# Scattering the lists of experts 2 to 7 earlier, reading them a step later, and products on TensorE that nobody reads

## The chip, the cores and the metric

The kernel runs on one core of one Trainium2 chip. The metric is the device time of one execution in microseconds; several timed runs give a median.

## The reference

Three stages follow each other. The input is a batch of 4 sequences of 448 tokens with 12 heads of 64 (1792 tokens of 768 values).

```python
# attention, per head: q, k normalised by their root mean square, softmax, times v
x = attention(q, k, v)                     # [1792, 768]
# first mixture of experts, 8 experts, cap = 1792 / 8 = 224 tokens each
order = argsort(-(x @ w_gate).flatten())   # best (token, expert) pairs first
for tok, e in order:                       # a token goes to the first expert with room
    if assigned[tok] < 0 and counts[e] < cap: assigned[tok] = e; counts[e] += 1
for e in range(8): out[assigned == e] = relu(x[assigned == e] @ w1[e]) @ w2[e]
# second mixture: expert = argmax(x @ w_gate2 + bias[modality]), any count,
# rows scaled by the softmax weight of the chosen expert
```

## The kernel before, in words

Attention writes its rows to a table x_d in DRAM. Then comes the routing of the first mixture: a search by rounds for one threshold for each expert (`one_round`), after which `choose` writes the 0/1 matrix `Dm` (token by expert) and `ranks` writes `rk`, each token's place in its expert's list. `judge` counts the tokens of each expert and writes a flag. Code behind `tc.If(f1 > 0)` (line 1005) repairs the choice where the flag is set; every engine reads the flag and passes the branch. With these inputs the body isn't run.

The lists say which tokens an expert gets. Those of experts 0 and 1 are worked out on TensorE: `slots1` compares `rk` with the slot numbers on VectorE, `slots2` multiplies by token numbers on TensorE, and `gather1` has GpSimd fetch the 224 rows of x by two indirect DMAs. Those of experts 2 to 7 go through DRAM: `lists` (five VectorE operations) turns `rk` and `Dm` into positions `pos1`; `lists_go` has GpSimd scatter (token, modality) pairs, one indirect DMA for each of the 16 chunks of 112 tokens, into three zeroed tables `l1_d` in turn (`c % 3`), so that a scatter writes the same table as the third before it and waits for it; `list_load` has SyncE read the three tables back, and VectorE add them to `idx` and `inf`.

The experts then run one after the other, a step `u` for each: 8 steps of the first mixture, then steps of the second over tiles of tokens. A step has 16 chunks. Chunks 0 to 7 are `layer1` (18 products of 224 columns each in split precision, into one of three PSUM tiles `ph`), chunks 8 to 15 are `layer2`. Between them an order written out by hand places everything else: `at(u, c, f)` runs f after the products of chunk c of step u and ahead of their copies out of PSUM (`layer1_end`, `layer2_end`), and with `late=True` behind these copies. Each engine runs its instructions in that order. So placed are the weight loads on SyncE (`w_load`, four buffers `raw`), their splits into high and low parts on ScalarE and VectorE (`w_split`), the gathers, the transposes of the next step's rows into `xs` (`x_turn`, chunks 10 to 15), and the routing of the second mixture.

Just ahead of step 0, behind `judge`, VectorE has the six low parts of w1 (line 1003 with 806), then the branch, then its share of `x_turn(0)`.

In the order of before the lines that matter here are:

```python
at(0, 3, slots2, 1, oh1)
at(0, 3, lists, late=True)
at(0, 5, lists_go, 0, 8)
at(0, 8, lists_go, 8, NCH)
at(0, 15, list_load)
...
cg = 4                      # chunk of gather(1) in step 0; gather(2) is at chunk 3 of step 1
```

Of the kernel before, what the change touches and what calls it, by code (L numbers as in the profile page):

```python
# [8 lines left out]
FT = mybir.dt.float32  # L9
FR = mybir.dt.float32r  # L10
HF = mybir.dt.float16
I32 = mybir.dt.int32
AF = mybir.ActivationFunctionType
OP = mybir.AluOpType
# [13 lines left out]
def build(ctx, tc, q, k, v, g_q, g_k, m1_gate, m1_w1, m1_w2, modality, m2_gate, m2_bias, m2_w1, m2_w2,  # L28
# [5 lines left out]
    P = 112  # L34
# [911 lines left out]
    def gather1(e):  # L946
        for t in range(2):
            nc.gpsimd.indirect_dma_start(out=XG[e][:P, t], out_offset=None, in_=x_d,
                                         in_offset=bass.IndirectOffsetOnAxis(ap=IDX[e][:, t, 0:1], axis=0))
# [4 lines left out]
        IDX[e], INF[e] = idx[:, 2 * e:2 * e + 2], inf[:, 2 * e:2 * e + 2]  # L954


    XR2 = []

    def rows_last(c):
# [36 lines left out]
    slots(0)  # L996
    XG[0] = io.tile([128, 2, HD], FT, name="xg")
    gather1(0)
    judge(0)
    nc.vector.tensor_reduce(add4, ident.rearrange("p (a c) -> p c a", a=4)[:, :E], axis=AX.X, op=OP.add)  # L1000
    nc.vector.memset(flag_i[:, 1:3], 0)
    for i in range(DJ):
# [2 lines left out]
    with tc.If(f1 > 0):  # L1005
        with tc.For_i(0, 4, 1) as _i:
            one_round()
        choose()
        judge(1)
        f2 = nc.values_load(flag_i[0:1, 1:2], min_val=0, max_val=4096)  # L1010
        with tc.If(f2 > 0):
            for f in spread(NCH, mm, mc, mcb, sm[:, 0], lambda: ps1.tile([128, 512], FT, name="ph")):
                f()
            with tc.For_i(0, 40, 1) as _i:
                one_round()
            choose()
            judge(2)
            f3 = nc.values_load(flag_i[0:1, 2:3], min_val=0, max_val=4096)
            with tc.If(f3 > 0):

                fid = rr.tile([P, NCH, E], FT, name="fid")
                for b in range(B):
                    nc.gpsimd.iota(fid[:, b * CPB:(b + 1) * CPB], pattern=[[E, CPB], [1, E]], base=b * S * E,
                                   channel_multiplier=CPB * E, allow_small_or_imprecise_dtypes=True)
                nc.vector.tensor_copy(vv, lg)
                nc.vector.memset(Dm, 0.0)
                cnt = sm[:, 0, :]
                nc.vector.memset(cnt, 0.0)
                col = rr.tile([P, 4], FT, name="col")
                row = rr.tile([1, P], FT, name="row")  # L1030
                one = rr.tile([1, 1], FT, name="one")
                hs = rr.tile([P, E], HF, name="hs")

                def top(src, c):

                    p1 = ps1.tile([128, 512], FT, name="ph")
                    nc.tensor.transpose(p1[:1, :P], src, ident[:P, :P])
                    nc.vector.tensor_reduce(one, p1[:1, :P], axis=AX.X, op=OP.max)
                    nc.vector.tensor_copy(row, one.to_broadcast([1, P]))
                    p2 = ps1.tile([128, 512], FT, name="ph")  # L1040
                    nc.tensor.matmul(p2[:P, 0:1], row, ident[0:1, 0:1], start=True, stop=True)
                    nc.vector.tensor_copy(col[:, c:c + 1], p2[:P, 0:1])

                with tc.For_i(0, N, 1) as _i:
                    fl2 = vv.rearrange("p c e -> p (c e)")
                    nc.vector.tensor_reduce(col[:, 0:1], fl2, axis=AX.X, op=OP.max)
                    top(col[:, 0:1], 1)
                    nc.vector.tensor_scalar(lt0, vv, col[:, 1:2], None, op0=OP.is_equal)
                    nc.vector.tensor_scalar(uu, fid, -1.0, 20000.0, op0=OP.mult, op1=OP.add)
                    nc.vector.tensor_mul(uu, uu, lt0)  # L1050
                    nc.vector.tensor_reduce(col[:, 2:3], uu.rearrange("p c e -> p (c e)"), axis=AX.X, op=OP.max)
                    top(col[:, 2:3], 3)
                    nc.vector.tensor_scalar(lt0, uu, col[:, 3:4], None, op0=OP.is_equal)
                    nc.vector.tensor_add(Dm, Dm, lt0)
                    nc.vector.tensor_reduce(mx, lt0, axis=AX.X, op=OP.max)
                    nc.vector.tensor_scalar(mx, mx, -2e38, 1e38, op0=OP.mult, op1=OP.add)
                    nc.vector.tensor_tensor(vv, vv, mx[:, :, None].to_broadcast([P, NCH, E]), op=OP.min)
                    nc.vector.tensor_reduce(sm[:, 1, :], lt0.rearrange("p c e -> p e c"), axis=AX.X, op=OP.add)
                    nc.vector.tensor_copy(hs, sm[:, 1, :])
                    p3 = ps1.tile([128, 512], FT, name="ph")  # L1060
                    nc.tensor.matmul(p3[:, :E], ones_h[:P], hs, start=True, stop=True)
                    nc.vector.tensor_add(cnt, cnt, p3[:P, :E])
                    full = sm[:, 2, :]
                    nc.vector.tensor_scalar(full, cnt, float(cap) - 0.5, None, op0=OP.is_gt)
                    nc.vector.tensor_scalar(full, full, -2e38, 1e38, op0=OP.mult, op1=OP.add)
                    nc.vector.tensor_tensor(vv, vv, full[:, None, :].to_broadcast([P, NCH, E]), op=OP.min)
        ranks()
        slots(0)
        gather1(0)
    rr_st.close()  # L1070


# [109 lines left out]
            layer2_end(u, c - 8)  # L1182
        run(16 * u + c, True)


    pos1 = act.tile([P, NCH], I32, name="p3i")

    def lists():
        p3 = act.tile([P, NCH, E], FT, name="p3")
        ps = act.tile([P, NCH], FT, name="p3s")  # L1190
        e224 = act.tile([P, 1, E], FT, name="e224")
        nc.vector.tensor_scalar(e224, eio[:P], float(cap), -1.0, op0=OP.mult, op1=OP.add)
        nc.vector.tensor_add(p3, rk, e224.to_broadcast([P, NCH, E]))
        nc.vector.tensor_mul(p3, p3, Dm)
        nc.vector.tensor_reduce(ps, p3, axis=AX.X, op=OP.add)
        nc.vector.tensor_copy(pos1, ps)

    def lists_go(a, b):
        for c in range(a, b):

# [10 lines left out]
    def slots_next(a):  # L1211
# [2 lines left out]
            OH.append(act.tile([P, HD], mybir.dt.bfloat16, name="junk").bitcast(HF))  # L1214
        slots1(1, a, a + 4, oh1)

    def list_load():
        l3 = act.tile([P, 3, 2 * E, 2], I32, name="l3")
        for g in range(3):
            nc.sync.dma_start(l3[:, g, 4:], l1_d[g][2 * cap:].rearrange("(t p) f -> p t f", p=P))  # L1220
        nc.vector.tensor_add(l3[:, 0, 4:], l3[:, 0, 4:], l3[:, 1, 4:])
        nc.vector.tensor_add(idx[:, 4:], l3[:, 0, 4:], l3[:, 2, 4:])
        nc.vector.tensor_copy(inf[:, 4:], idx[:, 4:, 1])
# [211 lines left out]
    for u in range(US):  # L1435
        if u < E:
            W[u] = (m1_w1[u], m1_w2[u])
            at(u, 3 if u == E - 1 else 9, route_bias, u)
        for p in range(3, 7):
            for i in range(2):  # L1440
                c = 2 * (p - 3) + i
                at(u, c, w_split, u, p, i, nc.vector)
        nx = u + 1
        if u == 0:
            for p in range(4, 7):
                at(0, -1, w_load, 0, p)
            for i in range(4):
                at(0, i // 2, slots_next, 4 * i, late=True)
            at(0, 3, slots2, 1, oh1)
            at(0, 3, lists, late=True)  # L1450
            at(0, 5, lists_go, 0, 8)
            at(0, 8, lists_go, 8, NCH)
            at(0, 15, list_load)
        if u < E:
            route(u)
        if u in (E - 2, E - 1):
            if u == E - 2:
                at(u, 0, tile_consts)
            at(u, 9, tile_pick, u - E + 2, late=True)
        if u == E:  # L1460
            for i, f in enumerate(tile_rest()):
                at(u, 7 + i // 5, f, late=True)
        if nx == US:
            break

        cv, cw, cs, cg, cx = None, (1, 3, 5), (8, 8, 9, 10, 10, 11), 3, range(10, 16)
        if u == 0:
            cg = 4
        elif nx >= E:
            cv = 0  # L1470
        if cv is not None:
            j = nx - E - NP0 - (NT0 if nx in SHORT else 0)
            at(u, cv, tile_values, nx, slice(j, j + 1))
        for p in range(3):
            at(u, cw[p], w_load, nx, p)
        if cv is not None:
            at(u, cw[0], tile_list, nx)
            at(u, cg, tile_gather, nx)
        else:
            at(u, cg, gather, nx)  # L1480
        at(u, max(7, cw[2]), w_load, nx, 3)
        for p in range(3):
            for i in range(2):
                at(u, cs[2 * p + i], w_split, nx, p, i, nc.vector)
            at(u, min(15, cs[2 * p + 1] + 1), w_load, nx, 4 + p)
        for j in range(DJ):
            at(u, cx[j], x_turn, nx, j)
# [53 lines left out]
```

## Time and profile before

| | us |
|---|---|
| median of three timed runs | 889.77 (886.84 to 889.78) |
| the profiled execution | 888.51 |
| its span in the profile | 886.7 |
| TensorE busy with products | 793.2 (89%) |
| VectorE busy | 570.6 (64%) |
| ScalarE busy | 466.7 (53%) |
| GpSimd busy | 138.9 (16%) |

The span runs from the first to the last recorded instruction; the profiled execution's own time has 1.8 us more around it. Engines are called PE (TensorE), PEld (its weight loads), DVE (VectorE), ACT (ScalarE), POOL (GpSimd) and SP (SyncE) in the rows; "SPq" and "DVEq" are their queues. TensorE's granted clock, PEclk, is given as a share of 2.4 GHz; 0.50 is 1.2 GHz.

### The profile page before, as it was taken

The page shows a single profiled execution, that of the slowest core. Times are in us where ns is not written, and L with a number is a line of the kernel's source. Part 1 is how long each engine was busy: PE and PEld are TensorE (multiplying, and loading weights), DVE is VectorE, ACT ScalarE, POOL GpSimd, SP SyncE. Part 2 cuts the span into 40 slices and gives each one's busy share as a digit, 9 for nine tenths or more (in the row PEclk, how much of TensorE's full clock was granted, in tenths as well). Part 3 has the DMA queues.
Part 4 walks back from the last instruction along what each step waited for, and adds up shares of the span by engine and source line. Part 5 has one row for each costly group of instructions (what it writes and reads, how often), then busy time and mean ns, then how long its engine had stood idle before and what let it go on. Part 6 is the DMA issues. An engine that isn't in the chain of part 4 may idle for free.

```text
span 886.7 us, 14891 instructions
## 1 busy us (share of the span) xinstructions
PE 793.2 (89%) x5611; PEld 655.8 (74%) x5611; DVE 570.6 (64%) x1196; ACT 466.7 (53%) x803; POOL 138.9 (16%) x230
## 2 busy tenths in 40 slices
PE   1689999999753894999999999999999999999994
PEld 1323333333343894999999999999999999999983
DVE  5998898973588751736647456584865665655741
ACT  3667767754270351645546456464565555555641
POOL 4520000000022143101111031030110110110000
PEclk9899999999955796999999999999999999999997
DMA  8449699680171682767667576584875865865710
GB/s 195 99 98 212 162 205 228 159 171 21 51 254 32 228 215 48 224 190 235 192 204 237 186 227 192 172 257 171 264 235 188 289 214 182 287 203 203 261 63 18
DMA packets 113785, 161.22 MB, mean 182 GB/s; under 512 B 59328, under 2 KB 77248, under 8 KB 113696
## 3 DMA queue, kind: packets, MB, share of 16 engines
q1 hardware_dynamic: 108928, 143.07, 55.8%
q0 software_dynamic: 4768, 17.02, 5.6%
q8 instruction: 49, 0.80, 0.4%
q14 instruction: 40, 0.33, 0.1%
HBM read 128.78 MB, written 17.22 MB: 165 GB/s over the span
## 4 chain that ended last, share of the span: by engine, by line
PE 59%; DMA 3%; DVE 1%; ACT 1%; POOL 1%; issue 1%; SPq 0%; ACTq 0%; POOLq 0%; DVEq 0%
PE ph L1115 9%; PE py L1149 9%; PE py L1150 9%; PE py L1151 9%; PE ph L1116 9%; PE ph L1117 9%; DMA l_d<-tok,p3i 3%; PE pt L1100 2%; PE pt L1256 1%; DVE w2s L806 1%; PE pi L1266 1%; ACT w2s L804 1%; POOL l_d L1201 1%; DMA l<-l_d 0%; PE pi L1275 0%
## 5 line engine op out<-in xcount | busy, mean ns | idle before, releaser
L1116 PE MATMUL ph<-xs,w1s 128*128 128x224 f32 (+1 forms) x720 | 200.4, 278 | 12.7 <-DVE xs L1102 12.7
L1115 PE MATMUL ph<-xs,w1s 128*128 128x224 f32 (+1 forms) x720 | 204.9, 285 | 0.0
L1117 PE MATMUL ph<-xs,w1s 128*128 128x224 f32 (+1 forms) x720 | 200.1, 278 | 0.0
L1149 PE MATMUL py<-w2s,hh 128*112 128x384 f32 (+1 forms) x496 | 173.3, 349 | 1.3 <-ACT hh L1135 1.3
L1150 PE MATMUL py<-w2s,hl 128*112 128x384 f32 (+1 forms) x496 | 167.6, 338 | 0.0
L1151 PE MATMUL py<-w2s,hh 128*112 128x384 f32 (+1 forms) x496 | 167.3, 337 | 0.0
L806 DVE TENSOR_TENSOR w2s<-raw,w2s 128x768 fp32r<-128x768 f32 x128 | 122.5, 957 | 69.3 <-ACT w2s L804 69.2
L1116 PEld LDWEIGHTS ph<-xs,w1s 128*128 128x128 f32 x720 | 139.2, 193 | 12.8 <-DVE xs L1102 12.8
L1115 PEld LDWEIGHTS ph<-xs,w1s 128*128 128x128 f32 x720 | 139.0, 193 | 3.2 <-DVE hl L1136 2.5
L1117 PEld LDWEIGHTS ph<-xs,w1s 128*128 128x128 f32 x720 | 139.1, 193 | 0.0
L806 DVE TENSOR_TENSOR w1s<-raw,w1s 128x1024 fp32r<-128x1024 f32 x96 | 113.2, 1220 | 14.9 <-ACT w1s L804 14.9
L804 ACT ACTIVATE w2s<-raw 128x768 fp32r<-128x768 f32 x128 | 107.2, 838 | 0.0
L1102 DVE TENSOR_TENSOR xs<-pt,xs 128x224 fp32r<-128x224 f32 (+2 forms) x93 | 37.0, 398 | 105.0 <-ACT xs L1101 105.0
L804 ACT ACTIVATE w1s<-raw 128x1024 fp32r<-128x1024 f32 x96 | 96.6, 1058 | 0.8 <-DMA raw<-in_moe_w_dram 0.8
L1101 ACT ACTIVATE xs<-pt 128x224 fp32r<-128x224 f32 (+2 forms) x93 | 33.7, 362 | 114.5 <-PE pt L1100 87.4
L438 ACT ACTIVATE pp<-sc,gs 128x896 f32<-128x896 f32 x72 | 70.0, 1006 | 42.0 <-PE sc L431 41.7
L1149 PEld LDWEIGHTS py<-w2s,hh 128*112 128x112 f32 (+1 forms) x496 | 90.2, 182 | 2.2 <-ACT hh L1135 2.0
L1150 PEld LDWEIGHTS py<-w2s,hl 128*112 128x112 f32 (+1 forms) x496 | 90.4, 182 | 0.4
L1151 PEld LDWEIGHTS py<-w2s,hh 128*112 128x112 f32 (+1 forms) x496 | 90.2, 182 | 0.1
L1135 ACT ACTIVATE hh<-ph 128x224 fp32r<-128x224 f32 (+1 forms) x120 | 44.3, 369 | 81.4 <-PE ph L1117 80.6
L453 PE MATMUL av<-pp,vt 128*64 128x448 f32 x288 | 64.3, 554 | 0.0
L1136 DVE SCALAR_TENSOR_TENSOR hl<-ph,hh 128x224 fp32r<-128x224 f32 (+1 forms) x120 | 48.4, 403 | 19.9 <-ACT hh L1135 19.9
(306 smaller groups left out, 1075.7 us busy)
## 6 DMA issues: line engine op xcount, KB each, us to landing
raw<-in_moe_w_dram SPq DMA_DIRECT2D x48, 1024.0 KB, 5.0
raw<-in_moe_w_dram SPq DMA_DIRECT2D x64, 768.0 KB, 5.9
y_d<-yr SPq DMA_DIRECT2D x16, 336.0 KB, 4.1
qt<-in_q_dram SPq DMA_DIRECT2D x11, 448.0 KB, 5.0
kt<-in_k_dram SPq DMA_DIRECT2D x24, 192.0 KB, 3.4
vt<-in_v_dram SPq DMA_DIRECT2D x12, 384.0 KB, 4.3
qTs<-qT SPq DMA_DIRECT2D x20, 224.0 KB, 3.5
x_d<-xr SPq DMA_DIRECT2D x12, 336.0 KB, 3.0
```

The costliest lines, as they stand in the source:

```text
L438: nc.scalar.activation(PP[n][:, 2 * g:2 * g + 2, :] if g < 3 else P7[n], ps[:, :w, :S], AF.Exp, scale=gs[:, 4:5])
L453: nc.tensor.matmul(AV[n][64 * s:64 * s + 64, :S], LV[u][:, 3 * (2 * j + s) + g, :], pp[:, 2 * g + s, :], start=(g == 0), stop=False, skip_ ...
L804: nc.scalar.activation(d[:, 0, j, c], RAW[u, p][:, i, c], AF.Copy)
L806: eng.tensor_sub(d[:, 1, j, c], RAW[u, p][:, i, c], d[:, 0, j, c].bitcast(FT))
L1115: nc.tensor.matmul(ph[:, :n], wh, x[:, 0], start=a, stop=False)
L1116: nc.tensor.matmul(ph[:, :n], wh, x[:, 1], start=False, stop=False)
L1117: nc.tensor.matmul(ph[:, :n], wl, x[:, 0], start=False, stop=z)
L1135: nc.scalar.activation(hh, src, AF.Relu)
L1136: nc.vector.scalar_tensor_tensor(hl, src, 0.0, hh.bitcast(FT), op0=OP.max, op1=OP.subtract)
L1149: nc.tensor.matmul(py, a, wh, start=(f == 0), stop=False)
L1150: nc.tensor.matmul(py, b_, wh, start=False, stop=False)
L1151: nc.tensor.matmul(py, a, wl, start=False, stop=(f == FB - 1))
```

## The change

`lists` is computed right behind `judge`, ahead of the branch (and again inside the branch, where the choice is repaired). The first eight scatters are placed at chunk 0 of step 0, ahead of gather(1), and the last eight at chunk 6, behind it. The load of the tables moves to chunk 0 of step 1, and its sum, now a function of its own, to chunk 2 of step 1, ahead of gather(2) at chunk 3. Beside this `stay_warm` issues products on TensorE whose result nobody reads: three between `slots2` and `judge`, fourteen between `judge` and the transposes of the first rows. Each has 112 rows and 448 columns in f16 and reads the one-hot tile `ohs`.

```diff
+    pos1 = rt.tile([P, NCH], I32, name="p3i")
+    lp = rr.tile([P, NCH, E], FT, name="lp")
+    lsum = rr.tile([P, NCH], FT, name="p3s")
+    e224 = rr.tile([P, 1, E], FT, name="e224")
+
+    def lists():
+        nc.vector.tensor_scalar(e224, eio[:P], float(cap), -1.0, op0=OP.mult, op1=OP.add)
+        nc.vector.tensor_add(lp, rk, e224.to_broadcast([P, NCH, E]))
+        nc.vector.tensor_mul(lp, lp, Dm)
+        nc.vector.tensor_reduce(lsum, lp, axis=AX.X, op=OP.add)
+        nc.vector.tensor_copy(pos1, lsum)
+
+    def stay_warm(n):
+        pw = ps1.tile([128, 512], FT, name="ph")
+        for _ in range(n):
+            nc.tensor.matmul(pw[:, :4 * P], ones_h[:P], ohs[:, 0:2].rearrange("p c w -> p (c w)"), start=True, stop=True)
...
     gather1(0)
+    stay_warm(3)
     judge(0)
+    lists()
+    stay_warm(14)
...
         ranks()
         slots(0)
         gather1(0)
+        lists()
...
-    pos1 = act.tile([P, NCH], I32, name="p3i")
-    def lists():
...
     def list_load():
-        l3 = act.tile([P, 3, 2 * E, 2], I32, name="l3")
+        L3.append(act.tile([P, 3, 2 * E, 2], I32, name="l3"))
         for g in range(3):
-            nc.sync.dma_start(l3[:, g, 4:], l1_d[g][2 * cap:].rearrange("(t p) f -> p t f", p=P))
+            nc.sync.dma_start(L3[0][:, g, 4:], l1_d[g][2 * cap:].rearrange("(t p) f -> p t f", p=P))
+
+    def list_sum():
+        l3 = L3[0]
         nc.vector.tensor_add(l3[:, 0, 4:], l3[:, 0, 4:], l3[:, 1, 4:])
         nc.vector.tensor_add(idx[:, 4:], l3[:, 0, 4:], l3[:, 2, 4:])
         nc.vector.tensor_copy(inf[:, 4:], idx[:, 4:, 1])
...
             at(0, 3, slots2, 1, oh1)
-            at(0, 3, lists, late=True)
-            at(0, 5, lists_go, 0, 8)
-            at(0, 8, lists_go, 8, NCH)
-            at(0, 15, list_load)
+            at(0, 0, lists_go, 0, 8)
+            at(0, 6, lists_go, 8, NCH)
+            at(1, 0, list_load, late=True)
+            at(1, 2, list_sum, late=True)
```

## Rows read from the trace of the kernel before

**Rows 1.** The page: busy tenths and clock in 40 slices.

```profile
PE   1689999999753894999999999999999999999994
PEclk9899999999955796999999999999999999999997
```

**Rows 2.** Stretches: steps 0, 1 and 2; columns as the heading names them.

```profile
core 0: us, PE busy (x) PEld busy (x) DVE busy (x) ACT busy (x) POOL busy (x), PEclk, DMA share, GB/s
293.30:332.10 38.80, 38.78 (x291) 38.54 (x291) 24.20 (x53) 18.54 (x34) 12.73 (x13) 0.93 0.73 206
332.10:384.85 52.75, 40.09 (x288) 39.05 (x286) 21.61 (x47) 19.88 (x38) 12.51 (x24) 0.84 0.50 147
384.85:421.64 36.79, 36.79 (x287) 35.91 (x286) 21.14 (x44) 19.89 (x38) 6.17 (x11) 1.00 0.66 210
```

**Rows 3.** Timeline of TensorE: start, length, instruction, idle before and releaser.

```profile
293.33 0.53 PE L1115 MATMUL ph<-xs,w1s 128*128 128x224 f32 x1
...
320.00 0.36 PE L1100 MATMUL pt<-ident,xg 112*128 112x112 f32 x2
...
332.11 0.35 PE L1115 MATMUL ph<-xs,w1s 128*128 128x224 f32 x1
...
346.79 0.56 PE L1116 MATMUL ph<-xs,w1s 128*128 128x224 f32 x1 [12.65 <-DVE xs L1102]
```

**Rows 4.** Timeline, 341 to 347 us: the load and the sum.

```profile
341.12 2.80 SPq L1220 DMA_DIRECT2D l<-l_d  x3
...
344.89 0.18 DVE L1221 CUSTOM_DVE_ANT_0 l<-l 112x48 uint16<-112x48 uint16 x1 [13.85 <-DMA l<-l_d]
```

**Rows 5.** Timeline of GpSimd: gather(1), then the 16 scatters.

```profile
306.17 0.94 POOL L948 DMA_INDIRECT xg<-x_d,idx  x1 [20.20 <-DVE inf L940]
...
308.64 0.97 POOL L1201 DMA_INDIRECT l_d<-tok,p3i  x1 [0.30 <-issue]
309.92 0.95 POOL L1201 DMA_INDIRECT l_d<-tok,p3i  x1 [0.30 <-issue]
...
338.13 0.94 POOL L1201 DMA_INDIRECT l_d<-tok,p3i  x1 [0.30 <-issue]
```

**Rows 6.** The chain of waits in order of time, 309 to 346 us.

```profile
309.92 8.92 DMA l_d<-tok,p3i
...
319.11 6.11 DMA l_d<-tok,p3i
...
338.13 2.90 DMA l_d<-tok,p3i
...
342.20 3.73 DMA l<-l_d
```

**Rows 7.** Stretches around the changes of clock; columns as in rows 2.

```profile
240.20:244.00 3.80, 0.00 (x0) 0.00 (x0) 1.39 (x2) 0.00 (x0) 0.26 (x1) 1.00 0.22 20
...
290.10:293.30 3.20, 2.80 (x11) 1.79 (x12) 2.01 (x5) 1.43 (x5) 0.00 (x0) 0.50 1.02 376
293.30:298.50 5.20, 5.18 (x25) 5.20 (x25) 2.31 (x6) 2.10 (x5) 0.00 (x0) 0.50 0.31 118
...
334.10:336.20 2.10, 0.04 (x1) 0.00 (x0) 0.00 (x0) 0.00 (x0) 1.51 (x2) 1.00 0.02 1
...
346.80:353.10 6.30, 6.30 (x30) 6.30 (x31) 1.26 (x2) 1.97 (x5) 1.96 (x2) 0.50 0.42 109
```

**Rows 8.** Timeline, 283 to 292 us: judge, splits of w1, first copy.

```profile
283.11 0.16 PE L903 MATMUL ph<-ck,ones_h 112*128 112x1 f16 x1 [0.82 <-DVE ck L902]
...
285.06 5.76 DVE L806 TENSOR_TENSOR w1s<-raw,w1s 128x1024 fp32r<-128x1024 f32 x5
...
290.12 0.45 PE L1100 MATMUL pt<-ident,xg 112*128 112x112 f32 x1 [2.16 <-DMA xg<-x_d,idx]
...
291.47 0.36 ACT L1101 ACTIVATE xs<-pt 128x224 fp32r<-128x224 f32 x1 [27.01 <-DVEq L1005]
```

**Rows 9.** The tile p3i (pos1): landing of its 16 scatters.

```profile
DMA to landing us min/median/max: 2.1/4.2/9.3
```

**Rows 10.** Timeline of VectorE: lists from first operation to what follows.

```profile
306.38 0.16 DVE L1192 TENSOR_SCALAR e<-eio 112x8 f32<-112x8 f32 x1
...
307.63 0.95 DVE L806 TENSOR_TENSOR w2s<-raw,w2s 128x768 fp32r<-128x768 f32 x1
```

More of the change, by code (lines that the diff above doesn't have):

```diff
@@ L1183, in chunk @@
         run(16 * u + c, True)
-    pos1 = act.tile([P, NCH], I32, name="p3i")
-    def lists():
[L1189 to L1196, printed above, removed]
     def lists_go(a, b):
@@ L1215, in slots_next @@
         slots1(1, a, a + 4, oh1)
+    L3 = []
     def list_load():
-        l3 = act.tile([P, 3, 2 * E, 2], I32, name="l3")
+        L3.append(act.tile([P, 3, 2 * E, 2], I32, name="l3"))
         for g in range(3):
-            nc.sync.dma_start(l3[:, g, 4:], l1_d[g][2 * cap:].rearrange("(t p) f -> p t f", p=P))
+            nc.sync.dma_start(L3[0][:, g, 4:], l1_d[g][2 * cap:].rearrange("(t p) f -> p t f", p=P))
+    def list_sum():
+        l3 = L3[0]
         nc.vector.tensor_add(l3[:, 0, 4:], l3[:, 0, 4:], l3[:, 1, 4:])
```

## The prediction

> **What bounds the kernel now.** I read the busy slices of the page first. TensorE is at nine tenths or more in nearly every slice from the first quarter on, except in slices 11 to 14 and in slice 16 [rows 1]. In slices 12 to 14 and 16 its granted clock is below full as well. The kernel is therefore bound by TensorE's stream of products, and the questions are what opens these two holes and what each costs.
>
> The second hole lies in step 1 of the first mixture of experts. Steps 1 and 2 do the same work on TensorE, yet step 1 takes 52.75 us and step 2 takes 36.79 [rows 2]. The difference is 15.96 us. In the timeline TensorE begins step 1 at 332.11 and then stands 12.65 us before a product that starts at 346.79, released by VectorE's xs [rows 3]. VectorE itself stood 13.85 us at line 1221, the sum of the three lists, waiting for their load; SyncE issues that load only at 341.12 [rows 4]. The load waits for the scatters of line 1201: GpSimd issues the first at 308.64 and the last at 338.13 [rows 5], and the chain of waits shows the last landing 2.90 us after its start [rows 6]. Some of the scatters are slow because each writes the table that the third before it wrote: where the weight loads fill the DMA engines, the chain holds one landing of 8.92 us [rows 6]. The rest of the 15.96 is clock: after the stop TensorE runs 6.3 us at 0.50 (1.2 GHz) before it is back at 2.4 GHz [rows 7]. Half of that is 3.15 us, and 12.65 + 3.15 = 15.80, within 0.2 of the difference.
>
> The first hole is the routing stage. TensorE's clock is at 0.50 there, and remains so for the first 5.2 us of step 0's products [rows 7]; this costs 2.6 us. What the first product waits for is not TensorE: ScalarE's first copy of xs waits until 291.47 for VectorE to pass the branch of line 1005 [rows 8], and VectorE gets there only after its six subtractions on w1s, five of which run from 285.06 for 5.76 us [rows 8].
>
> **The change, part by part.**
>
> *The scatters start earlier.* They can't start before VectorE has passed the branch if they wait as ScalarE does, which is 291.5 plus what the change adds there (1.65, below): 293.2. The lower bound is when lists are done, near 285 (where the subtractions start now [rows 8]); I take 293.2, since pos1 is also written inside the branch. A scatter costs GpSimd 1.25 us from issue to issue where nothing holds it (308.64 to 309.92 is 1.28) [rows 5]. Where the third before must land first, a round of three takes one landing: median 4.2, at most 9.3 [rows 9]. At the median the first eight need two rounds and two issues, 293.2 + 8.4 + 2.5 = 304. gather(1), now queued behind them, was issued at 306.17, when its indices came, so it is not late [rows 5]. The last eight follow it from about 310.3 (gather(1) itself moves with step 0, 1.65 later, and its two halves take 1.25 each). Of these eight the first three find their tables free; with one round of 8.92 and one of 6.11 under the loads, the two landings that the chain shows there [rows 6], the last starts near 327 and lands by 333; before it landed at 341.0.
>
> *The load and the sum move into step 1.* SyncE now issues the three loads after the y rows of step 0. Step 1 begins at about 332.1 + 1.65 = 333.8, so these issue near 335, and with the 4.8 us that they took (341.12 to the end of the last landing, 342.20 + 3.73) [rows 4, 6] they are in by 340. VectorE reaches the sum after three chunks of products, roughly 6.5 us into the step, about 340.3. Behind the sum on VectorE stand hl and the w2 subtractions; three PSUM buffers let TensorE run on three chunks more, to about 347.5, before it misses them. Behind the load on SyncE stand the w1 loads of step 2, which are not needed before chunk 8. gather(2) is then issued near 341 and its rows are wanted ten chunks into the step, after 353. So the whole stall goes: **-15.95 us**. The cover is 7 us wide.
>
> *Five operations of lists on VectorE.* They now stand in front of the six subtractions and so on the path to the first xs. In step 0 they took from 306.38 to 307.63, 1.25 us, hidden there under TensorE [rows 10]: **+1.25**. Removing them from step 0 gives nothing, because TensorE was the bound.
>
> *Three products before judge.* No row has a 112 by 448 f16 product. In the low clock 25 products of 224 columns take 5.2 us, 0.21 each [rows 7], so 448 columns cost 0.42; by the same rate in the high clock half, 0.21. Three cost 1.25 us. Judge's last product started at 283.11 after an idle time of 0.82 [rows 8], which takes up that much. The rest, **+0.4**, reaches VectorE, since lists follow judge there. The bounds are 0 (if the clock had risen by then) and 1.25.
>
> *Fourteen products after judge.* 14 x 0.42 = 5.9 us from 283.6, so until 289.5. The second half of the rows of gather(0) is waited for until 290.12 [rows 8], so nothing behind them on TensorE is late: 0. If the clock rises meanwhile they end sooner.
>
> *What they buy.* Full clock from the first product would be worth the 2.6 us above; nothing is the other bound. Between the last unread product (289.5 at the latest) and the first real one (about 295) there are at least 5.5 us in which TensorE has only twelve transposes. The clock fell 2.1 us after TensorE stopped at 334.1 and 3.8 us after it stopped at 240.2 [rows 7]; and 2.80 us of transposes in the 3.2 us ahead of step 0 didn't raise it [rows 7]. Both speak for a clock that is back at 1.2 GHz when the products begin, so I take **0**. The Trainium skill has a rule that speaks against this part of the change: in "TensorE: Matmul & The Clock Gate", section "HAM oscillation — how this bites in real kernels", a wait between two bursts of products puts the clock back, and each next burst begins slow. The trace agrees with it at 334.1 and 240.2. By that rule the sum stays 874.2; if the transposes in the gap were enough to hold the clock it would be 871.6, and no row here shows such a gap.
>
> The sum: -15.95 + 1.25 + 0.4 = -14.3. The profiled execution took 888.51 with a span of 886.7, so 874.2 with a span near 872.4. The 888.51 lies between the fastest timed run, 886.84, and the median, 889.77; I forecast **874** for the median after.
>
> **The rivals.**
>
> *The clock holds (0.2).* The unread products raise the clock early and the transposes keep it. For it: TensorE would have work almost without a gap from the products of slots2 to 289.5. Against it: the two falls above. Time: 874.2 - 2.6 = 871.6; with quicker transposes about 871.
>
> *The lists come late all the same (0.15).* If every landing took 8.9 us, the round of three being the pace, the eighth scatter would go at 312.3 and gather(1) at 313.5 and 314.8; its rows were turned at 320.00 before [rows 3], 13.8 us after its first issue at 306.17 [rows 5], so a landing of up to 6 us costs nothing there and one of 9.3 about 3 us. The sixteenth would start at 337.8, land at 346.7, the load end at 351.5. TensorE, covered to 347.5, would stand 4 us and probably lose the clock: 4 + 3.2 = 7.2, so 881.4. For it: the landings under the weight loads. Against it: between 293.3 and 298.5 the DMA engines are busy for 0.31 of the time [rows 7], and the median landing is 4.2.
>
> *The end on the other side (0.03): slower.* The one mechanism is the same chain of landings with its price above the stall removed. The gain of 14.3 is used up when TensorE stands 11.1 us (plus 3.2 of clock), so until 358.6; the list loads take 4.8, so the last scatter must land at 353.8. From 293.2 that is 60.6 us for six rounds, 10.1 us for each. The longest landing was 9.3 [rows 9]. Past 10.8 a round it would be over 893, slower by more than 0.5%.
>
> *The added VectorE work hides after all (0.02)*, because something later than it holds the first xs: 888.5 - 15.95 = 872.6.
>
> The forecast case has 0.6 and its own range is 872 to 877, from +0 to +1.25 for the three products and about a microsecond each way for when the clock rises. To take in the clock that holds and most of the late lists, the range is 870.5 to 879.5. A difference under 0.5%, 4.4 us, is about what a measurement of this kernel can't tell from no change. Faster by more than that is all of the first and second cases and nearly all of the late lists: 0.95. Within it 0.02, slower 0.03.
>
> **What would show it.** Right: no TensorE wait of over 1 us in the first chunk of step 1, step 1 near 36.8 us, the last scatter starting before 330, the wait of 13.85 gone from VectorE. The first product of step 0 at about 295, 1.65 later, and about 5 us at 0.50 after it. Wrong: VectorE waiting several us at the sum (the landings), GpSimd issuing gather(1) after 310, a clock of 1.00 at the first product, or a first product no later than 293.3.

## The result, and the profile after

The changed kernel takes 880.64 us in the median of five runs (878.91 to 882.02), the kernel before 886.84 in five runs beside them (886.08 to 889.78). The ratio is 0.9918, with an interval of 0.9893 to 0.9942: faster by 6.2 us, 0.7%. The forecast was 874.0 in a range of 870.5 to 879.5. The sign was right, and more than half of the gain is missing.

The page after, the rows that answer to [rows 1]:

```profile
PE   1589999999944799999999999999999999999994
PEclk9889999999955799999999999999999999999998
```

The second hole is gone: slices 16 and 17 stand at nine tenths. The first is still there, with its low clock. The last slice had 7 tenths of the clock in [rows 1] and has 8 here; this is a piece of the last step at half clock in the profiled execution of before, worth 1.5 us. It is nothing that the change did: of the runs below, e7, e14 and e15 show it too (last steps of 37.5 us instead of 36.0), the last of them with the order of the changed kernel.

Stretches after: steps 0, 1, 2 and, below, full steps 9 to 13 of the second mixture together; columns as in [rows 2].

```profile
297.60:335.80 38.20, 38.18 (x289) 37.86 (x290) 23.16 (x48) 18.34 (x33) 17.91 (x23) 0.95 0.72 206
335.80:372.60 36.80, 36.80 (x286) 35.87 (x285) 21.58 (x47) 19.88 (x38) 8.27 (x11) 1.00 0.71 210
372.60:409.40 36.80, 36.80 (x286) 35.88 (x285) 21.14 (x44) 19.89 (x38) 5.09 (x11) 1.00 0.65 210
...
631.30:808.14 176.84, 176.84 (x1264) 175.82 (x1262) 102.13 (x140) 94.15 (x160) 22.10 (x20) 1.00 0.66 224
```

The same five steps of the kernel before:

```profile
643.04:815.38 172.34, 172.34 (x1264) 171.27 (x1262) 101.70 (x140) 94.15 (x160) 23.49 (x20) 1.00 0.68 229
```

Step 1 went from 52.75 to 36.8, so the stall is wholly gone. The surprise is the last pair of rows. In steps that the change doesn't touch, TensorE is busy without a gap in both kernels, runs the same 1264 instructions at a granted clock of 1.00, and needs 4.50 us more. Its groups by line and shape show which instructions these are; first the kernel before (layer 1, then layer 2), then the changed one (busy us and mean ns of one behind the bar):

```profile
L1115 PE MATMUL ph<-xs,w1s 128*128 128x256 f32 x241 | 67.0, 278 | 0.0
...
L1149 PE MATMUL py<-w2s,hh 128*128 128x384 f32 x160 | 56.0, 350 | 0.0
```

```profile
L1138 PE MATMUL ph<-xs,w1s 128*128 128x256 f32 x241 | 68.7, 285 | 0.0
...
L1172 PE MATMUL py<-w2s,hh 128*128 128x384 f32 x160 | 55.8, 349 | 0.0
```

Only the products of `layer1` are longer; the three lines of them have 241, 240 and 240 products, and 4.50 / 721 = 0.0062 us for each. In the timelines of TensorE they start 0.113 us apart before and 0.120 us apart after. Before:

```profile
684.74 0.28 PE L1115 MATMUL ph<-xs,w1s 128*128 128x256 f32 x1
684.85 0.28 PE L1116 MATMUL ph<-xs,w1s 128*128 128x256 f32 x1
684.96 0.28 PE L1117 MATMUL ph<-xs,w1s 128*128 128x256 f32 x1
685.08 0.28 PE L1115 MATMUL ph<-xs,w1s 128*128 128x256 f32 x1
```

After:

```profile
673.94 0.28 PE L1138 MATMUL ph<-xs,w1s 128*128 128x256 f32 x1
674.06 0.28 PE L1139 MATMUL ph<-xs,w1s 128*128 128x256 f32 x1
674.18 0.28 PE L1140 MATMUL ph<-xs,w1s 128*128 128x256 f32 x1
674.30 0.28 PE L1138 MATMUL ph<-xs,w1s 128*128 128x256 f32 x1
```

Now the stretch before step 0. VectorE before, the row of `rk` from which the routing's end is counted:

```profile
278.05 0.29 DVE L920 SCALAR_TENSOR_TENSOR rk<-ph,Dm 112x128 f32<-112x128 f32 x1 [1.20 <-PE ph L918]
```

VectorE after: `rk`, the first reading of judge, the first of lists and what follows them:

```profile
280.06 0.29 DVE L920 SCALAR_TENSOR_TENSOR rk<-ph,Dm 112x128 f32<-112x128 f32 x1 [1.20 <-PE ph L918]
...
286.27 0.17 DVE L904 TENSOR_SCALAR sm<-ph 112x8 f32<-112x8 f32 x1 [1.20 <-PE ph L903]
...
286.74 0.16 DVE L963 TENSOR_SCALAR e<-eio 112x8 f32<-112x8 f32 x1
...
288.00 0.20 DVE L1022 TENSOR_REDUCE add<-ident 128x8 f32<-128x32 f32 x1
```

TensorE after: the fourteen unread products, transposes, the first products of steps 0 and 1 (to [rows 3, 8]):

```profile
285.32 4.03 PE L973 MATMUL ph<-ohs,ones_h 112*128 112x448 f16 x14
...
292.07 0.32 PE L1123 MATMUL pt<-ident,xg 112*128 112x112 f32 x1 [1.98 <-DMA xg<-x_d,idx]
...
295.23 0.60 PE L1123 MATMUL pt<-ident,xg 112*128 112x112 f32 x2 [2.65 <-DVEq L1027]
...
297.62 0.52 PE L1138 MATMUL ph<-xs,w1s 128*128 128x224 f32 x1
...
335.85 0.35 PE L1138 MATMUL ph<-xs,w1s 128*128 128x224 f32 x1
```

Stretches of the clock after, to [rows 7]:

```profile
287.90:294.60 6.70, 2.25 (x12) 0.99 (x10) 6.69 (x9) 0.00 (x0) 0.00 (x0) 1.00 0.64 193
294.70:297.60 2.90, 1.99 (x8) 1.32 (x9) 1.64 (x6) 1.51 (x6) 1.92 (x2) 0.50 0.99 360
297.60:301.50 3.90, 3.88 (x18) 3.90 (x19) 1.69 (x3) 1.04 (x2) 1.80 (x2) 0.50 0.32 119
```

The unread products do raise the clock, but it is back at 0.50 three microseconds before the first product, and stays there for 3.9 us of products (5.2 in the profiled execution of before; but where the clock rises behind the first product varies between executions, see e3). From `rk` to the first product it is 15.28 us before (293.33 - 278.05) and 17.56 after. `rk` itself comes 2.01 us later in this execution; in the eight runs e1 to e8 it lies between 277.7 and 281.5 with and without the change, so that is not the change's doing.

GpSimd after, to [rows 5], and the landings of p3i's scatters, to [rows 9]:

```profile
295.36 0.97 POOL L1211 DMA_INDIRECT l_d<-tok,p3i  x1 [8.13 <-DVEq L1027]
...
306.02 1.02 POOL L1211 DMA_INDIRECT l_d<-tok,p3i  x1 [0.30 <-issue]
310.37 0.96 POOL L948 DMA_INDIRECT xg<-x_d,idx  x1 [3.34 <-DVE inf L940]
...
330.28 0.94 POOL L1211 DMA_INDIRECT l_d<-tok,p3i  x1 [0.30 <-issue]
```

```profile
DMA to landing us min/median/max: 3.0/5.6/8.1
```

The load and the sum after, to [rows 4]:

```profile
337.51 2.35 SPq L1232 DMA_DIRECT2D l<-l_d  x3
```

```profile
345.95 0.17 DVE L1236 CUSTOM_DVE_ANT_0 l<-l 112x48 uint16<-112x48 uint16 x1
```

The sum starts with no idle time before it. What changed between the two profiled executions, from the starts of the steps:

| stretch | before | after | difference |
|---|---|---|---|
| start to `rk` (varies between runs) | 278.05 | 280.06 | +2.01 |
| `rk` to the first product | 15.28 | 17.56 | +2.28 |
| step 0 | 38.78 | 38.23 | -0.55 |
| step 1 | 52.74 | 36.82 | -15.92 |
| steps 2 to 7 (rest of the first mixture) | 220.87 | 221.02 | +0.15 |
| steps 8 to 14 (second mixture) | 243.47 | 249.14 | +5.67 |
| last step (clock at the end of before) | 37.48 | 35.98 | -1.50 |

The sum is -7.86, and the spans differ by 886.7 - 878.8 = 7.9. The loss of 5.7 us in the second mixture has no counterpart in the prediction. The 0.55 of step 0 is not a gain that can be laid to the change: in the kernels below that have no unread product, step 0 takes anything from 37.50 us (e2) to 38.94 (e7).

### The profile page after: what moved, and what is told of

It reads as the page before. It is cut to its first block, busy times and chain, and to the rows that moved or that the text cites. A ratio compares the mean times of both kernels' runs of the same rounds, so it can differ in the third digit from the quotient of the medians.

```text
span 878.8 us, 14926 instructions
## 1 busy us (share of the span) xinstructions
PE 799.9 (91%) x5628; PEld 657.9 (75%) x5628; DVE 570.8 (65%) x1196; ACT 466.7 (53%) x803; POOL 137.7 (16%) x230
## 4 chain that ended last, share of the span: by engine, by line
PE 63%; ACT 1%; DVE 1%; issue 0%; POOL 0%; ACTq 0%; POOLq 0%
PE ph L1138 10%; PE py L1172 10%; PE py L1173 10%; PE py L1174 10%; PE ph L1140 10%; PE ph L1139 10%; PE pt L1123 2%; PE pt L1271 1%; DVE w2s L806 1%; PE pi L1281 1%; ACT w2s L804 1%; PE pi L1290 0%; DVE hs L1157 0%; ACT xs L1124 0%; POOL out_dram L1191 0%
```

## The experiments

What could slow products whose instructions, clock and neighbours are the same? The diff moves one tile of 64 bytes, `pos1`, from the pool `act` to the pool `rt`, which lies ahead of the weights. In the built programs everything between the two pools (the weight buffers raw, w1s and w2s, and the row buffers yr and xg) lies 64 bytes higher for it: w1s begins at byte 65312 of each partition instead of 65248, while xs stays at 177952. The first theory was therefore the place of the tiles; the rivals were the changed order (DMA traffic, the added instructions) and the unread products.

**e1: the changed kernel with pos1 elsewhere.**

```diff
-    pos1 = rt.tile([P, NCH], I32, name="p3i")
...
+    pos1 = io.tile([P, NCH], I32, name="p3i")
     choose()
```

> The changed kernel with one line moved: the tile pos1 lies behind the row buffers instead of in front of the weight buffers, so w1s and w2s lie where they lay before the change (65248 and 114400) and xs where it always lay. Theory, placement: the products of 256 columns in the second mixture follow each other at 0.113 us again instead of 0.120, a full step there takes 34.47 us instead of 35.37, and the median is 874.5 (873 to 876.5). Rival, the slower products have another cause (the clock, the transfers, the place of the instructions): the steps stay at 35.37 and the median at 880 to 881.

Measured 873.09 us (872.53 to 875.3), ratio 0.9846 [0.983, 0.9861]. Five full steps of e1 as a stretch:

```profile
628.63:800.97 172.34, 172.34 (x1264) 171.27 (x1262) 101.72 (x140) 94.14 (x160) 23.38 (x20) 1.00 0.68 229
```

To the hundredth the time of before, with the order of the changed kernel. The median is within 1 us of the forecast.

**e2: the kernel before with pos1 moved, and nothing else.** No instruction changes; only addresses do.

```diff
-    pos1 = act.tile([P, NCH], I32, name="p3i")
+    pos1 = rt.tile([P, NCH], I32, name="p3i")
```

> The kernel before with pos1 alone moved in front of the weight buffers: w1s and w2s lie 64 bytes higher, xs where it lay; no instruction is added, removed or moved. Theory, placement: the steps of 256 columns take 35.37 us and the median rises by 6 us, to 892 to 894. Rival, another cause in the change itself: no difference from the kernel before, 886.5 to 888, steps at 34.47.

Measured 894.33 us (891.53 to 897.74), ratio 1.0084 [1.0057, 1.0111]: some 7 us slower. Its five steps:

```profile
643.71:820.55 176.84, 176.84 (x1264) 175.82 (x1262) 102.09 (x140) 94.14 (x160) 21.18 (x20) 1.00 0.67 224
```

The time of the changed kernel, without any of its work. With e1 this shows the cause of the missing microseconds; the order and the unread products have no part in it. The runs e3, e4, e8, e9 and e12 below, which leave w1s and xs where they lay before, all have full steps of 34.47 us too.

**e3: e1 without the unread products.**

```diff
-    stay_warm(3)
     judge(0)
     lists()
-    stay_warm(14)
```

> The first experiment's kernel without the 17 unread products. Theory (they buy nothing, since the clock is back at its low level when the first rows are multiplied, and three of them hold up judge by 0.95 us): 0.5 to 1.5 us faster than the first experiment, about 873.5, the first product of step 0 1.25 us later after rk than before the change instead of 2.28, and 3 to 6.5 us of low clock behind it. Rival (they bring the return of the full clock forward): 1 to 2 us slower than the first experiment.

Measured 872.64 us (871.57 to 874.29), ratio 0.9832 [0.9817, 0.9846], not to be told from e1. From `rk` to the first product it takes 16.53 us, which is 15.28 plus the 1.25 of lists; in e1 it is 16.86. Step 0 takes 38.84 against 38.29 in e1. The 0.33 that the products cost ahead of step 0 is well beyond the spread of this stretch in kernels without them (15.18 to 15.29 in the order of before). The 0.55 that they seem to win in step 0 isn't: without them it lies between 37.50 and 38.94 (e2, e5, e6, e7, e10, e13, e14 and this run), according to when the clock rises behind the first product. So a gain from them is not shown.

**e4: the kernel before with the unread products alone.**

```diff
     gather1(0)
+    stay_warm(3)
     judge(0)
+    stay_warm(14)
```

> The kernel before with the 17 unread products alone. Theory: 0 to 1.5 us slower than the kernel before, 887 to 888.5, the first product about 0.95 us later after rk. Rival: 1 to 2.5 us faster, if the products of step 0 start at the full clock.

Measured 888.57 us in 12 runs (886.62 to 891.22), ratio 1.0018 [1.0007, 1.003]: if anything slower. Step 1 keeps its stall, at 52.12 us. The whole gain of the change comes from moving the scatters and their reading.

**e5, e6, e7: which place matters.** On the kernel before, e5 puts 64 bytes ahead of both w1s and xs, e6 lets xs alone slide down by 64 (pos1 created behind it), and e7 puts 448 bytes ahead of xs.

```diff
     inf = rt.tile([P, 2 * E], FT, name="inf")
+    pad = rt.tile([P, NCH], I32, name="pad")
+    nc.vector.memset(pad, 0)
```

```diff
-    pos1 = act.tile([P, NCH], I32, name="p3i")
...
         x_turn(0, j)
+    pos1 = act.tile([P, NCH], I32, name="p3i")
```

```diff
     pos1 = act.tile([P, NCH], I32, name="p3i")
+    pad = act.tile([P, 7 * NCH], I32, name="pad")
+    nc.gpsimd.memset(pad, 0)
```

> The kernel before with 64 unused bytes (and one short memset) in front of the weight buffers: w1s and xs both lie 64 bytes higher, so their distance is that of before. If the slow products come from the place of w1s alone, the full steps of the second mixture take 35.37 us, as in the second experiment; if they come from where w1s and xs lie to each other, 34.47 as before. The time: 892 to 894 or 886.5 to 888.

> The kernel before with pos1 laid behind xs instead of in front of it: xs alone lies 64 bytes lower, every other large tile where it lay, no instruction changed. xs and w1s then begin at the same place within 1024 bytes, as after the change, while w1s lies where it was fast. Place of w1s alone: 34.47 us for a full step, 886.5 to 888. Place of the two to each other: 35.37, 892 to 894.

> The kernel before with xs 448 bytes higher, 512 bytes from w1s within 1024 bytes. If the distance of the two sets the pace, the step differs from 35.37; whether it stays at 34.47 or falls below (products 0.107 apart, 33.7 us) is open, as is whether the products of 224 columns (36.79 us a step) move too. If w1s alone counts: 34.47.

One run each: 890.48, 892.38 and 894.91 us, beside 887.05 (886.15 to 889.36). The five steps of e5, e6 and e7, a fence each:

```profile
643.25:818.32 175.07, 175.07 (x1264) 174.04 (x1262) 102.02 (x140) 94.10 (x160) 21.47 (x20) 1.00 0.68 226
```

```profile
642.93:820.00 177.07, 177.07 (x1263) 176.00 (x1262) 102.03 (x140) 94.12 (x160) 21.95 (x20) 1.00 0.67 223
```

```profile
643.96:820.95 176.99, 176.99 (x1263) 176.03 (x1262) 102.03 (x140) 94.06 (x160) 21.29 (x20) 1.00 0.67 223
```

e6 moves no weight and is as slow as e2, so w1s's own place can't be all that counts. e5 keeps the distance from w1s to xs and is slower than before, so the distance alone isn't either. e7 has 35.40 us a step, where the distance called for anything but 35.37 and w1s's own place for 34.47. Both ideas fell.

**e8, e9, e12: can the unread products hold the clock?** Three ways to fill the wait ahead of step 0, each on e1: 24 products of 224 columns between the transposes (e8), 34 instead of 14 products ahead of the branch (e9), 16 transposes of the identity ahead of the first rows' (e12).

```diff
         x_turn(0, j)
+        if j == 1:
+            pw = ps1.tile([128, 512], FT, name="ph")
+            for _ in range(24):
+                nc.tensor.matmul(pw[:, :2 * P], ones_h[:P], slot, start=True, stop=True)
```

```diff
-    stay_warm(14)
+    stay_warm(34)
```

```diff
+        if u == 0 and j == 0:
+            for _ in range(16):
+                nc.tensor.transpose(pt[:, :128], ident, ident)
         for t in range(nt):
             nc.tensor.transpose(pt[:, w * t:w * t + w], XG[u][:w, t, 128 * j:128 * j + 128], ident[:w, :w])
```

> The first experiment's kernel with 24 more unread products of 224 columns between the second and the third pair of transposes of step 0, where TensorE waits 2.6 us for VectorE to pass the branch. Theory, the clock falls in this gap, too late to be of use at the first product: with the gap filled it is still full at the first product, the 4.3 us at 1.2 GHz go, and the time is 1.5 to 2.5 us less than in the first experiment, 870.5 to 871.6. Rival, the transposes behind the filling lose the clock all the same: 872.5 to 873.5, with 3 to 6.5 us of low clock behind the first product.

> e1 with 34 instead of 14 unread products between judge and the transposes of the first rows, so that TensorE runs products nobody reads until about the end of the branch. Theory: the clock, raised by the first of them, is then still full at the first product of step 0, as it was in e8, but without the delay of e8, whose products stood behind two transposes that waited for the branch; step 0 takes about 36.3 us instead of 38.29, the first product comes 16.9 us after rk as in e1, and the time is about 871 (e1: 873.1). Rival: the unread products hold up the transposes of the first rows, because some of them still run at the low clock, and the first product comes 1 us or more later: 872 to 874, no gain that can be measured over e1.

> e1 with 16 more unread products on TensorE, transposes of the identity matrix into the PSUM tile of the first rows' transposes, issued behind the branch and ahead of these. They read nothing that VectorE writes, so they need not wait for VectorE to pass the branch, and TensorE passes the branch itself as early as in e1 (288.1). At 0.21 us each they fill 288.1 to 291.5, in which TensorE of e1 waits for rows that nobody can copy before 292.9. Theory: the gap without products shrinks to the last four us, the clock is still full at the first product, step 0 takes 36.25 us as in e8 instead of 38.29, and the first product comes no later than in e1, 16.5 to 16.9 us after rk: about 870.7 (e1: 873.1, e3: 872.6). Rival: the clock falls before the first product all the same, as it did in e9 (there 0.7 us before it): step 0 38.3 and 873. Second rival: the products run at the low clock, take 6.8 us and push the first copy past 295: 874 to 875.

| | median, us | ratio | `rk` to first product | step 0 |
|---|---|---|---|---|
| e1 | 873.09 | 0.9846 [0.983, 0.9861] | 16.86 | 38.29 |
| e8 | 875.67 | 0.9867 [0.9846, 0.9888] | 19.56 | 36.24 |
| e9 | 874.94 | 0.9866 [0.9848, 0.9883] | 18.51 | 37.55 |
| e12 | 874.64 | 0.9865 [0.9843, 0.9887] | 17.37 | 38.00 |

None beats e1. TensorE of e8, its fill and what follows:

```profile
292.80 3.97 PE L1510 MATMUL ph<-slot,ones_h 112*128 112x224 f16 x24 [2.08 <-DVEq L1027]
296.61 0.35 PE L1123 MATMUL pt<-ident,xg 112*128 112x112 f32 x2
...
297.30 0.35 PE L1138 MATMUL ph<-xs,w1s 128*128 128x224 f32 x1
```

The fill waits for VectorE to pass the branch (2.08 us), as the transposes do in e1 (2.60), and then stands in front of the transposes for 3.8 us. It does bring a full clock (step 0 has 36.24, below all that the kernels without unread products show), but 2.05 won is less than 2.70 lost. The medians lose more, 2.6 us; the profiled execution of e8, 872.38, is the fastest of its four. TensorE of e9 at the branch:

```profile
284.15 7.74 PE L972 MATMUL ph<-ohs,ones_h 112*128 112x448 f16 x34
295.15 0.40 PE L1123 MATMUL pt<-ident,xg 112*128 112x112 f32 x2 [3.26 <-PEq L1027]
```

Here 3.26 us pass between the last unread product and the first transpose, put down to TensorE's own passing of the branch. Stretches of e9 and of e12 from the last unread work to the first products:

```profile
291.90:295.10 3.20, 0.00 (x0) 0.00 (x0) 1.18 (x2) 0.00 (x0) 1.37 (x2) 1.00 1.00 323
295.10:296.70 1.60, 1.21 (x10) 0.99 (x10) 0.68 (x3) 1.07 (x4) 1.30 (x2) 1.00 0.93 344
297.40:300.10 2.70, 2.70 (x13) 2.70 (x14) 1.65 (x3) 1.09 (x2) 0.94 (x1) 0.50 0.04 11
```

```profile
288.50:291.90 3.40, 2.42 (x20) 2.09 (x20) 3.40 (x4) 0.00 (x0) 0.00 (x0) 1.00 0.46 117
291.90:293.30 1.40, 0.12 (x2) 0.00 (x0) 1.40 (x2) 0.00 (x0) 0.00 (x0) 1.00 1.14 405
293.30:296.40 3.10, 1.86 (x8) 1.31 (x8) 2.03 (x5) 1.31 (x5) 1.71 (x2) 0.50 0.92 326
```

In e9 the clock falls just ahead of the first product (297.40), in e12 at 293.3, 3.2 us ahead of it (296.45). My theory for both, that a shorter gap keeps the clock up, fell. The rivals were right that there is no gain over e1. e12's named the reason too, a clock that falls ahead of the first product; e9's did not, since the first product came 1.65 later than in e1 for the 3.26 us at the branch and not for products at the low clock. The chance named for "the clock holds" in the prediction was too kind to it.

**e10, e11: where the pace comes back.** e10 is the kernel before with 1024 bytes ahead of xs; e11 is the changed kernel with 64 bytes ahead of xs, which gives the places of e5.

```diff
     pos1 = act.tile([P, NCH], I32, name="p3i")
+    pad = act.tile([P, 16 * NCH], I32, name="pad")
+    nc.gpsimd.memset(pad, 0)
```

```diff
     HH, PY, LT2 = {}, {}, {}
+    pad = act.tile([P, NCH], I32, name="pad")
+    nc.gpsimd.memset(pad, 0)
```

> The kernel before with a pad of 1024 bytes ahead of xs, so that xs, hh and hl lie 1024 bytes higher and the weights where they were; one more memset on GpSimd. Theory: the pace depends on the place of xs against that of the weights in a pattern that repeats with 1024 bytes or a power of two below: products of 256 columns at 0.113 us, full steps of the second mixture of 34.47 us, time as before. Rival: 34.47 was a property of the exact places, and any other place of xs gives steps of 35.0 to 35.4, as the shifts by 64 and 448 bytes did: 4 to 7 us slower.

> The changed kernel with a pad of 64 bytes ahead of xs, so that w1s and xs both lie 64 bytes higher than in the kernel before and hold its distance. Theory (places count, not the order of the instructions): the same places as in e5 give the same steps, 35.0 us, products at 0.118, and some 2 us less than the changed kernel: about 878. Rival (distance alone counts): 34.47 and about 874. Second rival: no change against 35.37.

One run each: 887.87 and 875.68 us, beside 887.34 (886.25 to 888.42). The five steps of e10 and of e11:

```profile
643.94:816.27 172.33, 172.33 (x1263) 171.26 (x1262) 101.65 (x140) 94.09 (x160) 23.36 (x20) 1.00 0.68 229
```

```profile
628.53:803.60 175.07, 175.07 (x1264) 174.04 (x1262) 102.04 (x140) 94.03 (x160) 21.61 (x20) 1.00 0.68 226
```

The steps of both are as the theory of places had them: 1024 bytes more change nothing, and e11, in the order of the changed kernel, repeats the 175.07 of e5, in the order of before. The time of e11, one run, came 2.3 us below its forecast of 878.

**e13 to e16: the halves of 128 bytes.** A rule that fits all places up to e11: steps are slow (35.37 us and more) where w1s and xs begin in the same half of a stretch of 128 bytes, and take 34.47 or 35.01 where they don't. e13 and e14 put 128 and 32 bytes ahead of xs of the kernel before; e15 raises both tiles of the changed kernel to 128 above before; e16 raises its w1s to 128 and its xs to 64.

e13 and e14 are e10 with `2 * NCH` and `NCH // 2`. e15 is the changed kernel with the lines below; e16 has the first pad (`pad`) alone.

```diff
     pos1 = rt.tile([P, NCH], I32, name="p3i")
+    pad = rt.tile([P, NCH], I32, name="pad")
+    nc.gpsimd.memset(pad, 0)
...
     HH, PY, LT2 = {}, {}, {}
+    pad2 = act.tile([P, NCH], I32, name="pad2")
+    nc.gpsimd.memset(pad2, 0)
```

> The kernel before with a pad of 128 bytes ahead of xs: xs, hh and hl lie 128 bytes higher, the weights where they were. Theory (halves): what counts is in which half of a stretch of 128 bytes w1s and xs begin. In all runs so far steps of 34.47 and 35.01 us came with the two in different halves (before, e10; e5, e11) and steps of 35.37 to 35.40 with both in the same half (after, e2, e6, e7). By it this kernel has steps of 34.47, products at 0.113 us, and the time of before. Rival: the pattern repeats only with 1024 bytes, or the offsets matter one by one: steps between 35.0 and 35.4, 4 to 7 us slower.

> The kernel before with a pad of 32 bytes ahead of xs, so that xs begins on a multiple of 64, as it did in no run so far. The halves say nothing of this place. If the pace depends on how much of the two tiles' rows shares a half, the steps lie between 34.47 and 35.40, near 34.9; if only whole stretches of 64 bytes count, 34.47 or 35.40.

> The changed kernel with 64 bytes more ahead of the weights and 64 bytes ahead of xs: w1s, w2s, xs, hh and hl all lie 128 bytes higher than in the kernel before. Order and work are those of the changed kernel, with two small memsets on GpSimd at its start. Theory (halves): steps of 34.47 us and the 6 us back, 873 to 874, as e1. Rival (offsets one by one): steps of 35.0 to 35.4, 877 to 881.

> The changed kernel with 64 bytes more ahead of the weights alone: against the kernel before w1s lies 128 bytes higher and xs 64. Theory (halves): both begin in the same half again, 35.4 us, products at 0.120, about 879 to 880. Rival (the distance counts, or each further move loosens it): below 35.1.

Measured 891.34, 894.24, 875.59 (875.01 to 876.01 in four runs, ratio 0.986 [0.9837, 0.9882]) and 879.7 us, beside 888.06 (885.65 to 891.37). e16 has full steps of 35.33, as the halves said. e13 has 34.96 where they said 34.47: a miss, next to its rival's 35.0. e14 has 35.31, close to 35.40, the second of its cases; that the pace goes by the share of the rows in a common half, near 34.9, fell. e15 came 1.6 us above the upper end of its forecast. It changes its pace within one execution; its steps 10 and 12:

```profile
664.35:699.40 35.05, 35.05 (x255) 34.84 (x254) 20.38 (x28) 18.82 (x32) 4.37 (x4) 1.00 0.69 226
733.82:768.23 34.41, 34.41 (x255) 34.20 (x254) 20.34 (x28) 18.83 (x32) 4.79 (x4) 1.00 0.67 230
```

So the halves separate 35.3 and more from the rest, but say nothing of the steps between 34.4 and 35.1.

## Why the prediction was wrong

The step that failed is the sum itself: "-15.95 + 1.25 + 0.4 = -14.3", taken from a profile whose remaining steps were held to be unchanged. The diff's line that moves `pos1` from `act` to `rt` was costed nowhere: a term put at nothing without a reason. The runs show it as longer `layer1` products in the full steps of the second mixture (35.37 us a step for 34.47; e1 and e2). The moved line costs 5.7 us by the table, and the medians of the changed kernel and of e1 give 0.9918 against 0.9846 of before, about 6.4 us. With the terms as measured, 888.51 + 2.01 + 2.28 - 0.55 - 15.92 + 0.15 + 5.67 - 1.50 = 880.65, against 880.64 for the profiled execution; as the stretches cover the whole execution, this only books the time, and the cause rests on e1 and e2.

- *The stall of step 1, -15.95:* right, -15.92. SyncE issued the load 1.66 us into the step (forecast some 1.2) and VectorE reached the sum without waiting, though 10.1 us into the step (345.95) and not 6.5.
- *The scatters, from 293.2:* right. The first went at 295.36, released by VectorE's passing of the branch; less the 2.01 of this execution that is 293.35. The landings were slower than I took (median 5.6 us, not 4.2), the longest shorter (8.1, not 9.3). The last scatter started at 330.28, or 328.3 on the same scale, where I had 327. gather(1) waited for its indices (3.34 us), not for the scatters.
- *Lists, +1.25:* right, 286.74 to 288.00, and again in e3.
- *Three products before judge, +0.4:* within its bounds, mis-sized. VectorE's wait for judge rose from 0.25 us to 1.20 here (also in e8 and e12), which is 0.95, and to 0.43 in e1, e4 and e9, which is 0.18. What decides between the two isn't shown.
- *Fourteen products, 0 on the path:* right; TensorE's second transpose still waited for the second rows of gather(0), until 292.07.
- *What they buy, 0:* right. The clock fell at 294.7, after 6.70 us in which TensorE was busy for 2.25, as it fell behind the stops at 334.1 and 240.2 of before. Step 0, at 38.23, lies within what kernels without these products show. The rule cited there from the Trainium skill ("TensorE: Matmul & The Clock Gate", "HAM oscillation — how this bites in real kernels") agrees: a full clock at 287.9, 0.50 at 294.7.
- *Of the marks under "What would show it":* step 1 and the waits came as named; the first product came 2.28 later after `rk`, not 1.65; the clock stood at 0.50 for 3.9 us of products, not 5; the last scatter, "before 330", started at 330.28, and "gather(1) after 310" would have misled, since it was issued at 310.37 only because the whole execution ran 2 us late.

The rivals: "lists late" and the slower end did not happen, since the landings ended well ahead of the sum; that the 881.4 of the first of them lies near the measured 880.64 is chance. None of the cases held that a stage far behind the change could slow down, so the range had no room for it; the two ends would have needed a term for the place of tiles.

## What to carry to other kernels

When an edit creates, drops or moves a tile, look at where every later tile then lies, and after the run compare the spacing of the products in a stage that the edit doesn't touch, at the same granted clock: here 64 bytes ate 6 of 14 microseconds. Products that nobody reads would have to run right up to the first real one without standing in front of what that one waits for; no kernel here does both, and in none of five (e1, e4, e8, e9, e12) did they bring a measurable gain. The lowest median, not to be told from that of e1, is that of e3, without them: 872.64 us, 0.9832 [0.9817, 0.9846] of before. Moving the scatters to the start of step 0 and the read into step 1 takes 16 us out of step 1, 14.7 net in e3.

## What the runs showed of the hardware

The pace of products depends on where their two operands lie in SBUF, the memory that holds the tiles. Starts in bytes of a partition, and the mean full step of the second mixture (the stretch of five steps, by five); "half" is which half of a stretch of 128 bytes w1s and xs begin in:

| kernel | w1s | xs | halves | step, us |
|---|---|---|---|---|
| before, e1 | 65248 | 177952 | second, first | 34.47 |
| e10 | 65248 | 178976 | second, first | 34.47 |
| e15 | 65376 | 178080 | second, first | 34.66 (34.41 to 35.06) |
| e13 | 65248 | 178080 | second, first | 34.96 |
| e5, e11 | 65312 | 178016 | first, second | 35.01 |
| e14 | 65248 | 177984 | both second | 35.31 |
| e16 | 65376 | 178016 | both second | 35.33 |
| after, e2 | 65312 | 177952 | both first | 35.37 |
| e7 | 65248 | 178400 | both second | 35.40 |
| e6 | 65248 | 177888 | both second | 35.41 |

All five places in the same half give 35.3 or more, all others 35.01 or less on the mean. That is a pattern over ten places, found when the places up to e11 were known; it forecast the side of e13, e15 and e16 rightly and the size of e13 and e15 wrongly. The same rows fit as well by the distance: from w1s to xs it is a multiple of 128 bytes plus 64 in the five faster places, and plus 0, or 96 in e14, in the five slower ones; no run tells the two rules apart. Nor does a run move w1s alone: raw, w2s, yr and xg move with it, while e6 does move xs alone. What sets the finer steps, and why e15 changes within an execution, stays open, as does the mechanism. Only 256-column products of `layer1` show it clearly: full steps of the first mixture, with 224 columns, lie between 36.77 (e6) and 36.88 us (e13), and the group of `layer2` shown above has 350 and 349 ns.

The Trainium skill ("SBUF — State Buffer", section "SBUF: two separate sides") says that TensorE's access to SBUF never waits on anyone. It speaks of the other users of SBUF, and no run here shows on what the slower products wait, so the rule is neither borne out nor refuted. But whoever reads it as free placement would miss what the pair e2 and before shows: the same instructions, clock and order, and 4.50 us in 172.34 for another address.

Also unexpected: behind 34 unread products TensorE needed 3.26 us to pass the branch (e9), where the changed kernel, e1, e4 and e8, behind fourteen, show 0.45 us. That it was busy right up to the branch is not the reason. In e4 it was so until 291.2, nearly as late as in e9 (291.9), and the first transpose follows at once:

```profile
291.62 0.29 PE L1109 MATMUL pt<-ident,xg 112*128 112x112 f32 x1 [0.45 <-PEq L1014]
```

e9 was profiled once, and the cause stays open.
